# Earlier attention loads, sums and low parts on GpSimd, and two gates moved ahead, in a fused attention and two-FFN kernel

## The chip, the cores and the metric

The kernel runs on one core of one Trainium2 chip. The metric is the device time of one execution in microseconds. PE is the TensorE matmul engine, DVE is VectorE, ACT is ScalarE, POOL is GpSimd and SP is the engine that issues every DMA of this kernel.

## What is computed

Queries, keys and values are (8, 8, 576, 64): 8 sequences, 8 heads, 576 tokens, 64 wide; attention is within chunks of 64 tokens. Its output, 4608 rows of 512, goes through two feed-forward layers:

```python
x  = softmax(q @ k.T / 8) @ v                     # per chunk of 64
xn = (x - mean) / sqrt(var + 1e-6) * g_ln
x  = x + relu(xn @ w_ch1) @ w_ch2                 # 512 -> 2048 -> 512
h  = relu(x @ w_in)                               # 512 -> 1024
c  = sum(conv_w[k] * shift(h, k - 1) for k in range(3))  # along the sequence
out = (h * sigmoid(c)) @ w_out                    # 1024 -> 512
```

## The kernel before, in words

**Precision.** Every large product is done with both operands split into a high part in fp32r and a low part, the rest: `mm3` (L112) is three matmuls (L113 to L115). A high part is one copy on ACT, a low part one subtraction on DVE, both 128x512. The weights come as 64-bit floats and are brought to 32 bits by one ACT step (`a`, L133) and three DVE steps (`t` L139, `m` L145, `n` L151).

**First part (0 to about 490 us): attention and the first layer's `w_ch1`.** 36 tiles of 128 tokens; four tiles make a slab of 512 columns. A slab is multiplied by `w_ch1` by Strassen's scheme: seven products per pair of blocks (`product`, L585), each of 24 matmuls of 256 columns, in a fixed sequence of slots; ACT and DVE take the results out of PSUM (`u`, L611, L615 to L630) and SP stores them to DRAM (`hd`). The attention of the next tiles runs between the slots (`session`, L639). The seven weight operands of each of four blocks (numbers 0 to 3; 0 and 1 for the first half of `w_ch1`'s columns, 2 and 3 for the second) need sums of weight tiles: `Block.s` (L312), four per block.

**Start-up.** The order of the first steps is written out by hand in the table `START`: a letter for the step and a number for the tile or weight. W loads a weight tile, L loads queries and keys (and values) of an attention tile, `a t m n` bring a weight to 32 bits, g scales it by `g_ln` (ACT, L310), s is a Strassen sum, h and l the high and low part; S are a tile's scores (PE, L384), M their maximum (DVE, L400), E the eight exponentials (ACT, L410), R P C V X the rest of attention, B and y the normalisation's statistics (its power of -1/2 is the kernel's one arithmetic step on POOL, L451). What stands behind `|` is placed after slot 0, 1, 2 and so on of the first slab's products, a `/` between slots. Weight n belongs to block n // 4, sum n too; h and l n to block n // 7.

**Second layer (`w_ch2`), about 490 to 886 us.** `Down` p = 0 to 8, one per slab, takes 16 steps in `F_ORDER`; each loads `hr` from DRAM, splits it (`hh` on ACT L701, `hl` on DVE L702) and does 12 matmuls of 512 columns, all into four PSUM banks (even p: banks 0 to 3). The 32 pieces of `w_ch2`, `w_in` and `w_out` are loaded and split meanwhile by `Piece` through `cv_step` (L219), a pipeline of four stages: a, m, h, l. After a pass, `finish` (L773) adds the residual (four DVE adds, L159) and transposes four tiles on DVE into one buffer `x2T` (L779), each stored to DRAM before the next may overwrite it; `load_x2` and `split_x2` (ACT L109, DVE L110) bring the result back as the operand of the second pass.

**Second pass, from 886 us.** For each slab i and each f = 0 to 7 a `Gate` (L881): 12 matmuls into bank 4 + f % 4, then relu (ACT, `hb` L902, `cv` L906), the other two taps of the convolution (DVE, L917), tanh (ACT, L927), the product (DVE, `gt` L932) and its high (ACT, L947) and low part (DVE, L951). `step` (L957) writes these for three gates at a time:

```python
if old:  old.gated(); old.high()
if new:  new.relu()
if new2: new2.taps(); new2.tanh()
if old:  old.low()
```

so a new gate's relu stands on ACT behind the high part of the gate two before it. Split kk of the next slab's operand follows the step of gate f = x0 + kk. `outtile` (L871) is the last matmul with `w_out`.

Of the kernel before, what the change touches and what calls it, by code (L numbers as in the profile page):

```python
# [22 lines left out]
R3 g7 y0 l5 C3 z0 y1 h9 V3 X2 W9 W11 L4 W12 e0 l9 g4 z1 X3 W14 W13 W15 L5 h8  # L23
h7 B2 e1 B3 h6 u1 l7 v1 y3 l8 z3 s4 e3 y2 s6 z2 s5 e2 l6 h11 j0 u2 j1 u3
s7 u5 v3 u7 h10 l11 j2 l10 u6 v2 h12 v6 j3 l12 u4 v5 h13 v4 l13 v7
|
S4 S5 M4 M5 E4 L6 L7 a8 t8 a10 t10 m8 n8
/ E5 g8 a9 t9 m10 n10
/ g10 a11 a12 t11 t12 m9
/ a14 n9 t14 g9 m12  # L30
/ R4 P4 C4 h14 n12 m11 g12 n11 a13
# [13 lines left out]
def attn_moe_moe2(  # L45
# [115 lines left out]
    class Piece:  # L161
# [27 lines left out]
        def l(self):  # L189
            sub(self.dst[:, 1], self.src, self.dst[:, 0].bitcast(F32))  # L190
# [79 lines left out]
    class Block:  # L270
# [53 lines left out]

# [197 lines left out]
    with tc.manual_schedule():  # L522
# [20 lines left out]
        def one(step):  # L543
# [19 lines left out]
            elif kind == "L":  # L563
                at.L(i, late=i > 5)
# [149 lines left out]
        EARLY = 5  # L714
        F_ORDER = [f + 8 * i for f in range(8) for i in range(2)]
        dp = None
        for p in range(NS + 1):
            if p + 1 < NS:
                slabs[p + 1] = Slab(p + 1)
            for G in range(4):  # L720
                for s, (n, lag) in enumerate(SLOTS):
# [15 lines left out]
                    if p == NS - 1:  # L737
                        if (G, s) == (0, 5):
# [7 lines left out]
                            cv_load(2)  # L746
                        elif (G, s) == (2, 5):
# [3 lines left out]
                            cv_load(NF1)  # L751
# [55 lines left out]
        todo = [(p, f) for p in range(NS) for f in F_ORDER]  # L807
        downs = {0: down}
        xrs = {}
        ended = None  # L810
        for n, (p, f) in enumerate(todo):
            hh, hl = parts

            if f >= 8:
                ahead = p * 8 + f % 8 + 3
                if ahead < 8 * NS:
                    if ahead % 8 == 0:
                        downs[ahead // 8] = Down(ahead // 8)
                    downs[ahead // 8].load(ahead % 8)
            if n + 1 < len(todo):  # L820
                parts = downs[todo[n + 1][0]].split(todo[n + 1][1])
            if p == 0 and n % 4 < 3 or n % 2:
                cv_step()
            if ended is not None:
                finish(downs[ended], xrs[ended])
                ended = None
            if f == 4:
                xrs[p] = residual(downs[p])
            if late and f >= 8:
                late.pop(0)()  # L830
            downs[p].down(f, hh, hl)
            if f == NF1 - 1:
                ended = p
            if (p, f) == (0, 15):
                cv_rest()
                load_cw()
                wb_tags = [(wb_p, f"w1{kk}{i}") for kk in range(2) for i in range(7)]
                wb_tags += [(pbx, "wx0"), (pbx, "wx1")]
                for i in range(16):
                    pool, tag = wb_tags[i]  # L840
                    if i < 8:
                        add_wi(i // 4, i % 4, lambda pool=pool: pool, tag)
                    else:
                        add_wo(i - 8, lambda pool=pool: pool, tag)
                cv_load(4)
            if (p, f) == (6, 0):
                load_x2(0)
            if p == 6 and f in (8, 9, 10, 11):
                split_x2(0, f - 8)
        cv_rest()  # L850
        finish(downs[NS - 1], xrs[NS - 1])
        for fn in late:
            fn()
        dp.release()
        wa_p.release()


# [8 lines left out]
        for f in (7, 6, 5):  # L866
            ring(f)
# [165 lines left out]
```

## Time and profile before

| what | value |
|---|---|
| median of 3 runs | 1293.47 us (1290.34 to 1294.29) |
| profiled execution, its own time | 1292.32 us |
| its span, first to last instruction | 1290.5 us |
| PE busy | 1239.9 us, 96% |
| DVE busy | 744.1 us, 58% |
| ACT busy | 613.9 us, 48% |
| POOL busy | 78.0 us, 6% |
| mean granted TensorE clock | 0.976 |

Busy times are sums over the whole span; the stages differ much, so they are read by stage.

### The profile page before, as it was taken

What the parts mean: (1) busy time and instruction counts of PE and PEld (TensorE: products, weight loads), DVE (VectorE), ACT (ScalarE), POOL (GpSimd) and SP (SyncE); (2) the same over time, 40 slices, a digit from 0 to 9 for tenths busy, and PEclk for the clock granted to TensorE, in tenths of its full rate; (3) what the DMA queues carried; (4) which work ended last, traced back from release to release, by engine and by line L of the source; (5) the groups of instructions that cost most, each with busy time, mean ns of one, the idle gap of its engine ahead of it and who ended that gap; (6) DMA issues with size and microseconds to landing.
All of it is one profiled execution on the core that took longest, in us unless ns stands there. A gap on an engine that the chain in (4) does not pass through costs nothing.

```text
span 1290.5 us, 23238 instructions
## 1 busy us (share of the span) xinstructions
PE 1239.9 (96%) x9096; PEld 1080.4 (84%) x9096; DVE 744.1 (58%) x1430; ACT 613.9 (48%) x1510; POOL 78.0 (6%) x172
## 2 busy tenths in 40 slices
PE   5569999999999999999999999999999999999998
PEld 4469999999999987788888888888788888888887
DVE  7897557556565568567633443334875645665540
ACT  6776646556455345244322222222765555565541
POOL 0000000000000000000000000000121111121100
PEclk6589999999999999999999999999999999999999
DMA  9724645555454386676344445440121101211001
GB/s 269 209 103 160 209 160 186 188 175 210 158 197 151 120 284 244 189 269 234 117 143 153 163 155 179 155 162 34 33 66 58 57 18 58 66 38 36 25 25 49
DMA packets 127021, 177.70 MB, mean 138 GB/s; under 512 B 12736, under 2 KB 72128, under 8 KB 126912
## 3 DMA queue, kind: packets, MB, share of 16 engines
q1 hardware_dynamic: 126912, 176.22, 40.8%
q8 instruction: 71, 1.16, 0.4%
q14 instruction: 38, 0.31, 0.1%
HBM read 110.13 MB, written 66.06 MB: 137 GB/s over the span
## 4 chain that ended last, share of the span: by engine, by line
PE 84%; DVE 6%; DMA 5%; ACT 3%; SPq 1%; issue 1%; ACTq 0%; DVEq 0%
PE banks L113 27%; PE banks L114 26%; PE banks L115 26%; PE banks L384 3%; DMA rk<-in_k_dram 1%; DMA w<-in_moe_w_ch_dram 1%; PE banks L466 1%; DVE w L156 1%; PE banks L424 1%; DMA wd<-in_moe_w_ch_dram 1%; DVE hl L702 1%; DMA x2d<-x2T 0%; DVE w L151 0%; DVE u L159 0%; DVE w L145 0%
## 5 line engine op out<-in xcount | busy, mean ns | idle before, releaser
L113 PE MATMUL banks<-xc,w 128*128 128x256 f32 x1008 | 286.7, 284 | 11.2 <-DVE u L159 8.1
L114 PE MATMUL banks<-xc,w 128*128 128x256 f32 x1008 | 281.8, 280 | 0.0
L115 PE MATMUL banks<-xc,w 128*128 128x256 f32 x1008 | 281.7, 279 | 0.0
L701 ACT ACTIVATE hh<-hr 128x512 fp32r<-128x512 f32 x144 | 91.1, 632 | 257.0 <-PE banks L115 256.7
L702 DVE SCALAR_TENSOR_TENSOR hl<-hr,hh 128x512 fp32r<-128x512 f32 x144 | 99.3, 689 | 191.6 <-ACT hh L701 191.5
L113 PEld LDWEIGHTS banks<-xc,w 128*128 128x128 f32 x1008 | 192.1, 191 | 14.4 <-DVE u L159 8.7
L115 PEld LDWEIGHTS banks<-xc,w 128*128 128x128 f32 x1008 | 191.9, 190 | 0.0
L114 PEld LDWEIGHTS banks<-xc,w 128*128 128x128 f32 x1008 | 191.8, 190 | 0.0
L113 PE MATMUL banks<-w,hl 128*128 128x512 f32 x396 | 154.9, 391 | 0.0
L114 PE MATMUL banks<-w,hh 128*128 128x512 f32 x396 | 154.3, 390 | 0.0
L115 PE MATMUL banks<-w,hh 128*128 128x512 f32 x396 | 154.2, 389 | 0.0
L159 DVE TENSOR_TENSOR u<-banks,u 128x512 f32<-128x512 f32 x108 | 74.3, 689 | 113.6 <-ACT u L611 84.9
L917 DVE SCALAR_TENSOR_TENSOR cv<-hb,cw_sb,cv 128x510 f32<-128x510 f32 (+31 forms) x256 | 117.2, 513 | 0.6
L113 PE MATMUL banks<-xb,w 128*128 128x512 f32 x288 | 113.6, 395 | 1.8 <-ACT hb L902 1.4
L114 PE MATMUL banks<-xb,w 128*128 128x512 f32 x288 | 113.1, 393 | 0.0
L115 PE MATMUL banks<-xb,w 128*128 128x512 f32 x288 | 113.0, 392 | 0.0
L611 ACT COPY u<-banks 128x512 f32<-128x512 f32 x108 | 64.4, 596 | 99.4 <-PE banks L115 98.6
L410 ACT ACTIVATE pp<-banks,mx 128x64 f32<-128x64 f32 x288 | 86.8, 335 | 26.4 <-DVE x L438 18.7
L113 PEld LDWEIGHTS banks<-w,hl 128*128 128x128 f32 x396 | 74.4, 188 | 17.7 <-DVE hl L702 2.4
L115 PEld LDWEIGHTS banks<-w,hh 128*128 128x128 f32 x396 | 74.3, 188 | 15.5
L114 PEld LDWEIGHTS banks<-w,hh 128*128 128x128 f32 x396 | 74.3, 188 | 15.2
L904 POOL COPY hal<-hb 128x2 f32<-128x2 f32 x64 | 41.7, 652 | 730.0 <-ACT hb L902 730.0
(106 smaller groups left out, 2184.1 us busy)
## 6 DMA issues: line engine op xcount, KB each, us to landing
hd<-u SPq DMA_DIRECT2D x144, 256.0 KB, 3.2
hr<-hd SPq DMA_DIRECT2D x72, 512.0 KB, 3.7
w<-in_moe_w_ch_dram SPq DMA_DIRECT2D x27, 512.0 KB, 7.4
rv<-in_v_dram SPq DMA_DIRECT2D x36, 256.0 KB, 5.3
xd<-x SPq DMA_DIRECT2D x36, 256.0 KB, 2.2
xr<-xd SPq DMA_DIRECT2D x36, 256.0 KB, 4.2
x2d<-x2T SPq DMA_DIRECT2D x36, 256.0 KB, 2.0
x2r<-x2d SPq DMA_DIRECT2D x36, 256.0 KB, 3.7
```

Source lines behind the costliest of these rows:

```text
L113: nc.tensor.matmul(ps, ll, rh, start=first, stop=False, **kw)
L114: nc.tensor.matmul(ps, lh, rl, start=False, stop=False, **kw)
L115: nc.tensor.matmul(ps, lh, rh, start=False, stop=last, **kw)
L156: nc.vector.tensor_tensor(out=out, in0=a, in1=b, op=ALU.subtract)
L159: nc.vector.tensor_tensor(out=out, in0=a, in1=b, op=ALU.add)
L384: nc.tensor.matmul(ps[half(c), e, j, :], lt[half(e), j, c, :], rt[half(e), j, c, :], start=True, stop=True,)
L410: nc.scalar.activation(out=pp[:, j, e, :], in_=self.both[T][:, e, j, :], func=AF.Exp, scale=SCALE, bias=mx[:, e, j:j + 1], accum_out=sm[:, ...
L611: nc.scalar.copy(flat(t), bank[to])
L701: nc.scalar.activation(out=self.hh, in_=t, func=AF.Relu)
L702: nc.vector.scalar_tensor_tensor(out=self.hl, in0=t, scalar=0.0, in1=self.hh.bitcast(F32), op0=ALU.max, op1=ALU.subtract,)
L904: nc.gpsimd.tensor_copy(out=hal[:, f, :], in_=hb[:, 512:514])
L917: nc.vector.scalar_tensor_tensor(out=cv[:, a:e], in0=hb[:, a + tap:e + tap], scalar=cw_sb[:, tap, f:f + 1], in1=cv[:, a:e], op0=ALU.mult, ...
```

## The change

Five edits. In `START`, the queries and keys of tiles 4 and 5 are loaded before weights 9 and 11 (they were loaded behind 11 and behind 15), their values by new steps K behind weight 15; the scores, maximum and exponentials of tile 5 move from slots 0 and 1 to slot 2. The eight sums of blocks 2 and 3 are issued on GpSimd. The 32 low parts of `Piece` are issued on GpSimd. Loading of the pieces starts with five, then one per step, where it was two, then all of the rest at once. And `Gate(0, 0)` and `Gate(0, 1)` stand within the last down pass, behind its steps of f = 6 and f = 7; the splits of slab 1 move from gates 0 to 3 to gates 2 to 5. For that `hb` and `cv` lie in another pool and `hb` has three buffers instead of four.

```diff
-R3 g7 y0 l5 C3 z0 y1 h9 V3 X2 W9 W11 L4 W12 e0 l9 g4 z1 X3 W14 W13 W15 L5 h8
+R3 g7 y0 l5 C3 z0 y1 h9 V3 X2 L4 W9 L5 W11 e0 l9 g4 z1 X3 W12 W14 W13 W15 K4
+K5 h8 ...
 |
-S4 S5 M4 M5 E4 L6 L7 a8 t8 a10 t10 m8 n8
-/ E5 g8 a9 t9 m10 n10
-/ g10 a11 a12 t11 t12 m9
-/ a14 n9 t14 g9 m12
-/ R4 P4 C4 h14 n12 m11 g12 n11 a13
+S4 M4 E4 a8 t8 a10 t10 m8 n8 L6
+/ g8 a9 t9 m10 n10
+/ S5 M5 E5 g10 a11 a12 t11 t12 m9 L7
+/ R4 P4 C4 a14 n9 t14 g9 m12
+/ h14 n12 m11 g12 n11 a13
...
         def l(self):                                  # Piece
-            sub(self.dst[:, 1], self.src, self.dst[:, 0].bitcast(F32))
+            nc.gpsimd.tensor_tensor(
+                out=self.dst[:, 1], in0=self.src, in1=self.dst[:, 0].bitcast(F32), op=ALU.subtract
+            )
...
         def s(self, i):                               # Block
             y = self.y
+            if self.c:
+                self.s_gp(i)
+                return
...
+        def s_gp(self, i):
+            y = self.y
+            if i == 0:
+                self.sa = self.room(0, [128, 2, 512], F32)
+            if i == 3:
+                self.s4 = at.tile([128, 512], "s4", 1)
+            out, a, b, op = (
+                lambda: (self.sa[:, 0], y[2], y[3], ALU.add),
+                lambda: (self.sa[:, 1], self.sa[:, 0], y[0], ALU.subtract),
+                lambda: (y[2], y[0], y[2], ALU.subtract),
+                lambda: (self.s4, y[1], self.sa[:, 1], ALU.subtract),
+            )[i]()
+            nc.gpsimd.tensor_tensor(out=out, in0=a, in1=b, op=op)
...
-                at.L(i, late=i > 5)
+                at.L(i, late=i > 3)
+            elif kind == "K":
+                at.Lv(i)
...
-                            cv_load(2)
+                            cv_load(EARLY)
...
-                            cv_load(NF1)
+                            cv_load(5)
...
+            if p == NS - 1 and f in (6, 7):
+                step(Gate(0, f - 6))
...
-                self.hb = hb = pb.tile([128, 514], F32, tag="hb", bufs=4, name="hb")
-                self.cv = cv = pb.tile([128, 514], F32, tag="cv", bufs=3, name="cv")
+                self.hb = hb = pbx.tile([128, 514], F32, tag="hb", bufs=3, name="hb")
+                self.cv = cv = pbx.tile([128, 514], F32, tag="cv", bufs=3, name="cv")
...
-            x0 = min(2 * i, 2)
+            x0 = 2
...
-            for f in range(NF2):
+            for f in range(0 if i else BEGUN, NF2):
```

The lines of the changed kernel stand about 20 lower in the first part (L410 is L429, L310 is L312); of the gates, taps L917 is L878, `gt` L932 is L893, `x2T` L779 is L801.

The order of instructions on ACT in the start-up, from tile 4's exponentials on (x8 are the eight of one tile; w are weight tiles), before:

```order
L410 ACTIVATE pp,sm<-banks,mx 128x64 x8
L133 ACTIVATE w_774<-w_449 128x512
L133 ACTIVATE w_777<-w_451 128x512
L410 ACTIVATE pp,sm<-banks,mx 128x64 x8
L310 ACTIVATE w_774<-w_774,g_sb 128x512
L133 ACTIVATE w_774<-w_579 128x512
L310 ACTIVATE w_777<-w_777,g_sb 128x512
```

and in the changed kernel:

```order
L429 ACTIVATE pp,sm<-banks,mx 128x64 x8
L133 ACTIVATE w_743<-w_449 128x512
L133 ACTIVATE w_746<-w_451 128x512
L312 ACTIVATE w_743<-w_743,g_sb 128x512
L133 ACTIVATE w_743<-w_585 128x512
L429 ACTIVATE pp,sm<-banks,mx 128x64 x8
L312 ACTIVATE w_746<-w_746,g_sb 128x512
```

Tile 5's exponentials moved behind g8 and a9; tile 4's still stand ahead of a8 and a10.

POOL's queue of the changed kernel in the first part (rs is the normalisation's power, one per tile; L342 are the sums, L190 the first low parts):

```order
L470 TENSOR_TENSOR rs<-rs,mhalf 128x1 x4
L342 TENSOR_TENSOR w_896<-w_746 128x512
L342 TENSOR_TENSOR w_896<-w_896,w_743 128x512
L470 TENSOR_TENSOR rs<-rs,mhalf 128x1
L342 TENSOR_TENSOR w_746<-w_743,w_746 128x512
L342 TENSOR_TENSOR s_1039<-w_743,w_896 128x512
L470 TENSOR_TENSOR rs<-rs,mhalf 128x1
L342 TENSOR_TENSOR w_1105<-w_840 128x512
L342 TENSOR_TENSOR w_1105<-w_1105,w_807 128x512
L342 TENSOR_TENSOR w_840<-w_807,w_840 128x512
L342 TENSOR_TENSOR s_1149<-w_807,w_1105 128x512
L470 TENSOR_TENSOR rs<-rs,mhalf 128x1 x30
```

Before, this queue held the 36 powers one behind the other; now the sums s8 to s15 stand between the powers of tiles 3, 4, 5 and 6.

DVE where the second pass begins, before (xr are the residual adds of the last down pass, the first L917 the taps of gates 0 and 1):

```order
L159 TENSOR_TENSOR xr<-banks,xr 128x512 x4
L779 STREAM_TRANSPOSE x2T<-xr 128x512 x4
L110 TENSOR_TENSOR xb_10029<-x2r,xb_10027 128x512
L917 SCALAR_TENSOR_TENSOR cv<-hb,cw_sb,cv 128x510
L917 SCALAR_TENSOR_TENSOR cv<-hb,cw_sb,cv 128x511
L110 TENSOR_TENSOR xb_10029<-x2r,xb_10027 128x512
L932 SCALAR_TENSOR_TENSOR gt<-cv,hb 128x511
```

and in the changed kernel:

```order
L878 SCALAR_TENSOR_TENSOR cv<-hb,cw_sb,cv 128x510
L878 SCALAR_TENSOR_TENSOR cv<-hb,cw_sb,cv 128x511
L159 TENSOR_TENSOR xr<-banks,xr 128x512 x4
L801 STREAM_TRANSPOSE x2T<-xr 128x512 x4
L893 SCALAR_TENSOR_TENSOR gt<-cv,hb 128x511
L878 SCALAR_TENSOR_TENSOR cv<-hb,cw_sb,cv 128x510
L878 SCALAR_TENSOR_TENSOR cv<-hb,cw_sb,cv 128x511
L912 TENSOR_TENSOR Gl_10055<-gt,Gh_10054 128x511
L110 TENSOR_TENSOR xb_10066<-x2r,xb_10064 128x512
```

Gate 0's taps moved ahead of the last pass's four transposes; gate 0's product now stands right behind them, and the splits (L110) come two gates later.

## Rows read from the trace of the kernel before

**Rows 1.** The profile's page: busy time, and the chain that ended last.

```profile
PE 1239.9 (96%) x9096; PEld 1080.4 (84%) x9096; DVE 744.1 (58%) x1430; ACT 613.9 (48%) x1510; POOL 78.0 (6%) x172
...
PE 84%; DVE 6%; DMA 5%; ACT 3%; SPq 1%; issue 1%; ACTq 0%; DVEq 0%
```

**Rows 2.** Stages: length; PE, PEld, DVE, ACT, POOL busy; granted clock; DMA share, GB/s.

```profile
0.00:47.00 47.00, 26.95 (x320) 20.45 (x321) 37.28 (x79) 31.65 (x103) 3.62 (x12) 0.59 0.86 239
47.00:101.00 54.00, 34.56 (x495) 32.30 (x494) 46.06 (x92) 38.88 (x117) 1.79 (x2) 0.79 0.45 144
...
455.00:490.00 35.00, 30.21 (x261) 29.62 (x260) 22.55 (x38) 15.56 (x27) 0.00 (x0) 1.00 0.88 317
...
886.00:923.00 37.00, 35.21 (x147) 26.98 (x147) 25.69 (x39) 20.53 (x35) 2.65 (x9) 1.00 0.18 57
```

**Rows 3.** PE, 47 to 102 us: waits; in brackets idle time and its releaser.

```profile
58.05 1.64 PE L384 MATMUL banks<-rk,rq 64*64 64x64 f32 x32 [8.75 <-DMA rk<-in_k_dram]
...
84.27 0.58 PE L113 MATMUL banks<-xc,w 128*128 128x256 f32 x1 [5.36 <-DVE u L159]
...
97.59 2.10 PE L384 MATMUL banks<-rv,pt 64*64 64x64 f32 x64 [3.67 <-ACT pt L430]
```

**Rows 4.** DVE, same stretch: maximum of tile 5, sums s11 and s15.

```profile
59.76 0.69 DVE L400 TENSOR_REDUCE mx<-banks 128x8 f32<-128x512 f32 x1 [3.38 <-PE banks L384]
...
82.93 0.68 DVE L156 TENSOR_TENSOR s<-w,w 128x512 f32<-128x512 f32 x1
...
94.16 0.69 DVE L156 TENSOR_TENSOR s<-w,w 128x512 f32<-128x512 f32 x1
```

**Rows 5.** ACT, same stretch: a8 and a10, and two waits for sums.

```profile
58.80 1.25 ACT L133 ACTIVATE w<-w 128x512 f32<-128x512 f32 x2
...
83.70 0.62 ACT L335 CAST w<-w 128x512 fp32r<-128x512 f32 x1 [1.63 <-DVE s L156]
...
94.94 1.14 ACT L335 CAST w<-w 128x512 fp32r<-128x512 f32 x2 [2.71 <-DVE s L156]
```

**Rows 6.** POOL by line: busy time and mean; then one line's minimum, median, maximum.

```profile
L451 POOL TENSOR_TENSOR rs<-rs,mhalf 128x1 f32<-128x1 f32 x36 | 22.4, 623 | 404.7 <-DVE rs L450 397.2 <-DVE sm L417 7.5
masks.py:199 POOL TENSOR_SCALAR_AFFINE_SELECT ident<-ident 128x128 f32<-128x128 f32 x1 | 0.3, 292 | 0.1
...
L904 POOL COPY hal<-hb x64: 184/924/952, 889.9 to 1210.1; 128x2 f32<-128x2 f32 x64
```

**Rows 7.** PE before a product; DVE's L156 and L702 in the first down pass.

```profile
473.61 0.39 PE L113 MATMUL banks<-xc,w 128*128 128x256 f32 x1 [1.13 <-DVE u L159]
...
506.32 0.68 DVE L156 TENSOR_TENSOR w<-cy,w 128x512 fp32r<-128x512 f32 x1
...
509.32 0.69 DVE L156 TENSOR_TENSOR w<-cy,w 128x512 fp32r<-128x512 f32 x1
...
526.13 0.69 DVE L702 SCALAR_TENSOR_TENSOR hl<-hr,hh 128x512 fp32r<-128x512 f32 x1 [2.03 <-ACT hh L701]
528.85 0.69 DVE L702 SCALAR_TENSOR_TENSOR hl<-hr,hh 128x512 fp32r<-128x512 f32 x1 [2.03 <-ACT hh L701]
```

**Rows 8.** DVE where the second pass begins.

```profile
895.56 0.71 DVE L779 STREAM_TRANSPOSE x2T<-xr 128x512 f32<-128x512 f32 x1 [2.11 <-DMA x2d<-x2T]
...
900.11 0.68 DVE L932 SCALAR_TENSOR_TENSOR gt<-cv,hb 128x511 f32<-128x511 f32 x1
...
904.37 0.68 DVE L932 SCALAR_TENSOR_TENSOR gt<-cv,hb 128x511 f32<-128x511 f32 x1
...
911.77 0.69 DVE L932 SCALAR_TENSOR_TENSOR gt<-cv,hb 128x511 f32<-128x511 f32 x1 [0.41 <-ACT cv L927]
...
914.92 0.69 DVE L932 SCALAR_TENSOR_TENSOR gt<-cv,hb 128x511 f32<-128x511 f32 x1 [0.41 <-ACT cv L927]
```

**Rows 9.** ACT's relu of gates 0 and 2 in the same stretch.

```profile
889.28 0.60 ACT L902 ACTIVATE hb<-banks 128x512 f32<-128x512 f32 x1 [7.61 <-PE banks L115]
...
901.35 0.59 ACT L902 ACTIVATE hb<-banks 128x512 f32<-128x512 f32 x1
```

More of the change, by code (lines that the diff above doesn't have):

```diff
@@ L22 @@
 a7 t7 M2 m7 E2 n5 l3 S3 n6 m4 g5 P2 M3 g6 C2 n4 E3 V2 l4 n7 B1 h5 R2 P3
-R3 g7 y0 l5 C3 z0 y1 h9 V3 X2 W9 W11 L4 W12 e0 l9 g4 z1 X3 W14 W13 W15 L5 h8
-h7 B2 e1 B3 h6 u1 l7 v1 y3 l8 z3 s4 e3 y2 s6 z2 s5 e2 l6 h11 j0 u2 j1 u3
-s7 u5 v3 u7 h10 l11 j2 l10 u6 v2 h12 v6 j3 l12 u4 v5 h13 v4 l13 v7
-|
-S4 S5 M4 M5 E4 L6 L7 a8 t8 a10 t10 m8 n8
-/ E5 g8 a9 t9 m10 n10
-/ g10 a11 a12 t11 t12 m9
-/ a14 n9 t14 g9 m12
-/ R4 P4 C4 h14 n12 m11 g12 n11 a13
+R3 g7 y0 l5 C3 z0 y1 h9 V3 X2 L4 W9 L5 W11 e0 l9 g4 z1 X3 W12 W14 W13 W15 K4
+K5 h8 h7 B2 e1 B3 h6 u1 l7 v1 y3 l8 z3 s4 e3 y2 s6 z2 s5 e2 l6 h11 j0 u2
+j1 u3 s7 u5 v3 u7 h10 l11 j2 l10 u6 v2 h12 v6 j3 l12 u4 v5 h13 v4 l13 v7
+|
+S4 M4 E4 a8 t8 a10 t10 m8 n8 L6
[3 more added lines that the diff above has]
+/ h14 n12 m11 g12 n11 a13
 / R5 P5 C5 l14 t13 g11 m14 h15
@@ L714, in attn_moe_moe2 @@
         EARLY = 5
+        BEGUN = 2
         F_ORDER = [f + 8 * i for f in range(8) for i in range(2)]
@@ L806, in attn_moe_moe2 @@
         xb = [x_parts(pbx, "xb0")]
[L807 to L855, printed above, removed]
-        pb = tc.alloc_tile_pool(name="pb", bufs=1, reuse_waits="tile")
         RING = 1152
         Gh, Gl = {}, {}
-        def ring(f):
-            Gh[f] = pb.tile([128, RING], F32R, name=f"Gh{f}")
-            Gl[f] = pb.tile([128, RING], F32R, name=f"Gl{f}")
-        for f in (7, 6, 5):
-            ring(f)
-        for f in range(5):
-            ring(f)
-        xb.append(x_parts(pb, "xb1"))
         def outtile(T, tail=False):
@@ L969, in step @@
             flow[:] = new, new2
+        todo = [(p, f) for p in range(NS) for f in F_ORDER]
+        downs = {0: down}
+        xrs = {}
+        ended = None
+        for n, (p, f) in enumerate(todo):
+            hh, hl = parts
+            if f >= 8:
+                ahead = p * 8 + f % 8 + 3
+                if ahead < 8 * NS:
+                    if ahead % 8 == 0:
+                        downs[ahead // 8] = Down(ahead // 8)
+                    downs[ahead // 8].load(ahead % 8)
+            if n + 1 < len(todo):
+                parts = downs[todo[n + 1][0]].split(todo[n + 1][1])
+            if p == 0 and n % 4 < 3 or n % 2:
+                cv_step()
+            if ended is not None:
+                finish(downs[ended], xrs[ended])
+                ended = None
+            if f == 4:
+                xrs[p] = residual(downs[p])
+            if late and f >= 8:
+                late.pop(0)()
+            downs[p].down(f, hh, hl)
+            if f == NF1 - 1:
+                ended = p
+            if (p, f) == (0, 15):
+                cv_rest()
+                load_cw()
+                wb_tags = [(wb_p, f"w1{kk}{i}") for kk in range(2) for i in range(7)]
+                wb_tags += [(pbx, "wx0"), (pbx, "wx1")]
+                for i in range(16):
+                    pool, tag = wb_tags[i]
+                    if i < 8:
+                        add_wi(i // 4, i % 4, lambda pool=pool: pool, tag)
+                    else:
+                        add_wo(i - 8, lambda pool=pool: pool, tag)
+                cv_load(4)
+            if p == NS - 1 and f in (6, 7):
+                step(Gate(0, f - 6))
+            if (p, f) == (6, 0):
+                load_x2(0)
+            if p == 6 and f in (8, 9, 10, 11):
+                split_x2(0, f - 8)
@@ new lines, in attn_moe_moe2, with ring @@
+        cv_rest()
+        finish(downs[NS - 1], xrs[NS - 1])
+        for fn in late:
+            fn()
+        dp.release()
+        wa_p.release()
+        pb = tc.alloc_tile_pool(name="pb", bufs=1, reuse_waits="tile")
+        def ring(f):
+            Gh[f] = pb.tile([128, RING], F32R, name=f"Gh{f}")
+            Gl[f] = pb.tile([128, RING], F32R, name=f"Gl{f}")
+        for f in (7, 6, 5):
+            ring(f)
+        for f in range(5):
+            ring(f)
+        xb.append(x_parts(pb, "xb1"))
```

## The prediction

> **What bounds the kernel now.** I read the page first: PE is busy 1239.9 us of a span of 1290.5 and the chain that ended last lies on PE for 84% of the span [rows 1]. So only about 50 us can be won, and a queue that has slack costs nothing. The view by stages says where those 50 us lie [rows 2]: PE lacks 20.05 us before 47 us, 19.44 between 47 and 101, 4.79 between 455 and 490, and 1.79 between 886 and 923; elsewhere it is full but for some four at the very end. The change touches three of these four places, so I cost it stage by stage, each from the queue that PE waits for there.
>
> In the start-up I read PE's waits first, then the two engines that they name. PE sat 8.75 us for tile 5's keys, 5.36 for a DVE addition and 3.67 for an ACT copy [rows 3]. The first looks like the prize, but DVE idled only 3.38 us of it [rows 4]: behind that it runs back to back, 46.06 busy of 54 [rows 2]. DVE and ACT together set this stage, each waiting in turn for the other: ACT waited 1.63 and 2.71 us for the sums s11 and s15, which end on DVE at 83.61 and 94.85 [rows 4, 5].
>
> **Start-up, part by part.** *Loads.* SP issues eight small loads of queries and keys ahead of weights 9 and 11 and two loads of values later. The weights that they pass are wanted from about 60 us on, some ten microseconds behind their landing; nothing on PE, DVE or ACT waits for them. Tile 7's keys now start only behind tile 5's scores in slot 2; they keep a few microseconds. I cost the loads at nothing, with that cover named.
>
> *Tile 5 later.* M4 does not come earlier, since DVE is backlogged before it. With tile 5's maximum gone from there, DVE goes on to a8's conversion, and a8 stands on ACT behind tile 4's exponentials, whose end is at 58.80 [rows 5]. It gets a8 at about 59.45, while before it resumed at 59.76 [rows 4]: of the 3.38 us only 0.3 are won. The rest changes hands: tile 5's exponentials, which filled ACT from 60.76, now stand behind g8 and a9, and g8 waits for DVE's three conversion steps of 0.60 each. Walked on with the same durations, ACT idles about 2.85 us and tile 5's exponentials begin at about 63.95, and everything behind them comes some 1.3 us later.
>
> *Eight sums on GpSimd.* No operation of 128x512 on POOL is in the trace. Its nearest rows are one of 128x128 in 0.292 us and the power on one column in 0.62 us [rows 6]. Four times the columns of the first gives 1.17 us; the bounds are 0.62 (fixed cost alone) and 2.34 (if a second operand costs as much again). I take 1.17, by the row nearest in size. DVE loses 8 x 0.60 = 4.8 us of work, a low price; but the sums are on the path through POOL. s8 and s9 give DVE back 1.2 us, which about cancels the 1.3. s10 and s11 stand on POOL behind tile 4's power, which needs statistics that end at about 82.4 as before: 82.4 + 0.6 + 2 x 1.17 = 85.4 against 83.61, 1.8 us later for the copy that already waited for it [rows 5]. s12 to s15 wait for g15, now at about 90, and end at 90 + 4 x 1.17 = 94.7 against 94.85. Before, three of them ran together from 92.36 in 0.60 each behind other DVE work; now they start earlier and take longer. So the path ends where it did, within a few tenths. At 0.62 per sum it would end 2.2 us earlier, at 2.34 4.7 us later. DVE and POOL at work at once may also disturb each other: POOL's copy of two columns takes 0.184 us at best and 0.924 in the median [rows 6], where DVE works beside it, so POOL at least is held up. I take **+1.0** (−3 to +4.7) for the start-up.
>
> **Between the parts (455 to 520 us).** The wait of 2.06 us for the first piece's load stays, since it comes behind the same three `hr` loads. The wait of 1.13 us for a DVE addition [rows 7] had two low parts of 0.60 ahead of it on DVE; both go to POOL, so it goes. The later wait of 1.60 us has conversion steps ahead of it, which stay. In the first down pass DVE needs 3.00 us per step (506.32 to 509.32), PE 2.72 (526.13 to 528.85) [rows 7]; DVE was the slower one for nine steps but finished within PE's lead, so taking 0.60 of each step off DVE wins nothing there. Loading pieces one by one rather than eleven at once spreads DMA and costs nothing that I find. I take **−1.1** (−1.5 to +5, the upper end from the third rival).
>
> **Where the second pass begins (886 us).** Here is the largest term. Call T0 the end of the last down pass: gate 0's relu starts at 889.28, 2.72 behind it, so T0 = 886.56 [rows 7, 9]. DVE then does the residual adds and four transposes, each waiting 2.11 us for the store of the one before, until 896.27 = T0 + 9.71 [rows 8]. Only then come taps and gate products. PE does not mind: gates 0 to 3 have four free banks, and the relus of gates 0 and 1, which free banks 4 and 5, have no product of an older gate ahead of them on ACT. PE so has six gates, 16.3 us, to cover the transposes. The third relu ends at 901.94, which is 1.83 behind gate 0's product at 900.11 [rows 8, 9]. From there a step takes 4.26 us with a split of the next slab in it and 3.15 without [rows 8]. All in all PE loses little: 147 matmuls of 0.227 are 33.4 of 37.0 us [rows 2], some 3.5 lost.
>
> In the changed kernel gates 0 and 1 lie in the down pass, where ACT and DVE have room; PE's work is the same, the last pass ends at T = T0 + 5.44. The transposes start at T and end at T + 9.75, and gate 0's product stands behind them. The relu of gate 2 stands on ACT behind that product's high part, so it ends at T + 9.75 + 1.83 = T + 11.6. PE has four gates, 10.9 us, to cover this, not six: the two gates that needed nothing of DVE have been spent. Then come four steps with a split (gates 2 to 5, no longer 0 to 3): relus end at T + 15.8, 20.1, 24.4 and 28.6, then 31.8. The last split ends some 2.4 behind the relu of gate 5, at T + 26.8, and slab 1's first gate needs it: it ends at T + 27.5. Three more gates (the last two wait for relus at 28.6 and 31.8, hardly at all) end at T + 27.5 + 3 x 2.72 = T + 35.7. Ten gates are 27.2, so PE loses 8.5 against some 3.5: **+5.0**. Bounds: +3 if PE works on the splits as they come and the pace is nearer to 3.15 (two of the four pauses shrink by 1.1), +7 if TensorE's clock falls in the pauses of up to 4 us, as the granted clock of 0.79 shows for the stage with pauses of 5.36 and 3.67 us [rows 2, 3]. From 923 us on PE is full, so nothing gives this back.
>
> **Sum.** +1.0 − 1.1 + 5.0 = +4.9 on the profiled execution's 1292.32 us, which is 1297.2. That execution is 1.15 below the median shown, 1293.47; against it I say **1298.4 us**, 0.4% slower. About 0.3% (3.9 us) is what a measurement can tell from no change, so 1289.6 to 1297.4 counts as the same.
>
> **Rivals.** *DVE alone sets the start-up.* Then the whole 3.38 us and 8 x 0.60 are won, −8.2: 1293.47 − 8.2 − 1.1 + 5.0 = 1289.2, faster. For it: DVE's 46.06 of 54 us and ACT's waits of 1.63 and 2.71 for DVE's sums. Against it: a8 behind tile 4's exponentials, and g15, which POOL cannot pass. It decides where s15 ends on POOL: before about 91 us instead of 94.7. Chance 0.13.
>
> *The boundary is cheaper.* With +3 there, −2 in the start-up (short sums) and −1.1 it comes to −0.1: 1293.4, no change. For it: PE begins a gate on the first split. Against it: the transposes' end and the pace are measured. Chance 0.32, with the weaker mixtures of it.
>
> *DVE is held up by POOL.* If every DVE step with two operands waits for the POOL operation beside it, eight sums cost DVE 8 x (1.17 − 0.60) = 4.6 us and a down step takes 3.00 − 0.60 + 1.17 = 3.57 against PE's 2.72; nine steps lose 7.7, less the lead of some 2.5, so +5: 1293.47 + 4.6 + 5 + 5 = 1308. For it: POOL's copy of 0.184 that takes 0.924. Against it: no DVE row shows a wait for POOL. Chance 0.10. The Trainium skill (SBUF — State Buffer, Who interferes with whom) says that a DVE instruction with two SBUF inputs contends with a GpSimd instruction that reads SBUF, and that the later one is blocked for the whole of the other. By that rule this rival is the case; the trace agrees for POOL's side only. The GPSIMD Engine Reference (section 3.1) of the Trainium skill has 4497 ns for a sum of 2048 columns; a quarter, 1.12 us as an estimate, would give 94.5 for s15, no other sum.
>
> **How the numbers follow.** My forecast, slower by 2 to 9 us, has 0.45; with the contention rival's 0.10, slower by over 0.3% has 0.55. Within 0.3% 0.32, faster 0.13. The range reaches down to 1290.5, below the case of no change and near to that of the DVE-bound start-up, and up to 1305, between +7 at the boundary with +4.7 in the start-up and the contention case; beyond each end I leave about 1 in 10.
>
> **What would show it.** Start-up: PE's wait of 8.75 gone, tile 5's exponentials near 64, a sum of POOL near 1.17, s15's end near 94.7, PE full from about 101 as before. Middle: the wait of 1.13 gone. Boundary: DVE's gate product right behind the last transpose, PE waiting 8 us in all between the last down pass and gate (1,3). I am wrong if that loss is under 5 us, if s15 ends before 91, or if DVE shows waits for POOL of about a microsecond.

## The result, and the profile after

The changed kernel takes 1311.01 us (median of 4, 1310.39 to 1311.02), the kernel before 1293.3 beside it: ratio 1.0142 (95% interval 1.0129 to 1.0154), 17.7 us slower. I forecast 1298.4 in a range up to 1305. The direction was right, the size was not, and one effect of the other sign was not in the forecast at all.

In some executions, of the kernel before too, the 256-column matmuls of the whole first part follow each other every 117.7 ns instead of 113.5, which adds about 8 us; the traces of start_only and gates_only below are such executions, so their medians are compared and not their spans.

The profiled execution has a span of 1309.2 us against 1290.5. Busy time by stage, columns as in [rows 2], first two stages of the kernel before, which are not shown there:

```profile
490.00:540.00 50.00, 49.53 (x213) 38.55 (x212) 34.33 (x61) 22.88 (x38) 0.00 (x0) 1.00 0.54 171
...
900.00:950.00 50.00, 48.21 (x206) 37.94 (x206) 40.76 (x74) 34.86 (x61) 9.49 (x21) 1.00 0.16 48
```

and the changed kernel:

```profile
47.00:101.00 54.00, 32.97 (x369) 29.94 (x368) 43.75 (x76) 35.17 (x111) 12.86 (x10) 0.79 0.45 147
...
490.00:540.00 50.00, 44.52 (x198) 34.79 (x198) 37.55 (x46) 20.59 (x36) 14.38 (x11) 0.97 0.53 180
...
900.00:950.00 50.00, 43.25 (x173) 33.48 (x172) 33.97 (x55) 24.30 (x43) 4.61 (x13) 0.93 0.13 42
```

PE does less in the start-up, loses 5.5 us between 490 and 540 us (the end of the first part and the first down pass), where it lost half of one, and loses 6.75 where the second pass begins (1.8 before), with a granted clock of 0.93 there.

**Start-up.** PE, DVE, POOL and ACT of the changed kernel, where [rows 3 to 5] stand for the kernel before; the first line of DVE is tile 4's maximum, which began at 55.50 before:

```profile
66.97 1.11 PE L443 MATMUL banks<-ident,pp 128*128 128x128 f32 x4 [5.60 <-ACT pp L429]
...
102.48 0.69 PE L403 MATMUL banks<-rv,pt 64*64 64x64 f32 x32 [3.92 <-ACT pt L449]
```

```profile
56.11 0.69 DVE L419 TENSOR_REDUCE mx<-banks 128x8 f32<-128x512 f32 x1
...
60.16 0.69 DVE L145 SCALAR_TENSOR_TENSOR w<-w,w 128x512 int32<-128x512 int32 x1 [2.49 <-ACT w L133]
...
75.52 1.63 DVE L151 SCALAR_TENSOR_TENSOR w<-w,w 128x512 int32<-128x512 int32 x1
...
86.75 1.64 DVE L151 SCALAR_TENSOR_TENSOR w<-w,w 128x512 int32<-128x512 int32 x1
...
95.72 1.76 DVE L156 TENSOR_TENSOR w<-w,w 128x512 fp32r<-128x512 f32 x1
```

```profile
75.32 1.28 POOL L342 TENSOR_TENSOR w<-w,w 128x512 f32<-128x512 f32 x1
...
86.13 1.71 POOL L342 TENSOR_TENSOR s<-w,w 128x512 f32<-128x512 f32 x1
...
98.22 1.58 POOL L342 TENSOR_TENSOR s<-w,w 128x512 f32<-128x512 f32 x1 [1.30 <-DVE w L156]
```

```profile
87.88 0.62 ACT L354 CAST w<-w 128x512 fp32r<-128x512 f32 x1 [3.93 <-POOL s L342]
...
99.83 1.14 ACT L354 CAST w<-w 128x512 fp32r<-128x512 f32 x2 [3.63 <-POOL s L342]
```

The wait for the keys is gone and DVE waits 2.49 us for a8 instead, much as walked. A sum takes POOL 1.28 us, and up to 1.71 beside DVE; a DVE conversion step that overlaps one takes 1.63 instead of 0.69, a low part up to 1.76. s11 ends at 87.84 (83.61 before) and s15 at 99.80 (94.85). PE's product that waits for ACT's copy `pt` begins at 102.48 (97.59): 4.9 us lost. Of these, 0.6 were lost by tile 4's maximum already, ahead of all that the change moves on DVE; in the runs that leave the start-up as it was, it begins anywhere from 54.8 to 56.8.

**Ahead of the first down pass.** PE's last wait for a DVE addition, in the kernel before and in the changed one, and a conversion step of DVE ahead of it in the changed one:

```profile
487.74 0.39 PE L113 MATMUL banks<-xc,w 128*128 128x256 f32 x1 [1.60 <-DVE u L159]
```

```profile
494.78 0.39 PE L113 MATMUL banks<-xc,w 128*128 128x256 f32 x1 [2.66 <-DVE u L159]
```

```profile
491.09 1.51 DVE L139 TENSOR_SCALAR w<-w 128x512 int32<-128x512 uint32 x1
```

That step took 0.42 before; a low part runs on POOL beside it, and the wait is longer by the same 1.1.

**First down pass.** DVE, POOL and PE, against a step of 3.00 us before [rows 7]:

```profile
507.53 0.68 DVE L723 SCALAR_TENSOR_TENSOR hl<-hr,hh 128x512 fp32r<-128x512 f32 x1
508.13 0.42 DVE L139 TENSOR_SCALAR w<-w 128x512 int32<-128x512 uint32 x1
508.65 1.60 DVE L145 SCALAR_TENSOR_TENSOR cy<-cy,w 128x512 int32<-128x512 int32 x1
510.30 0.69 DVE L151 SCALAR_TENSOR_TENSOR cy<-w,cy 128x512 int32<-128x512 int32 x1
510.90 0.69 DVE L723 SCALAR_TENSOR_TENSOR hl<-hr,hh 128x512 fp32r<-128x512 f32 x1
```

```profile
508.39 1.31 POOL L190 TENSOR_TENSOR w<-cy,w 128x512 fp32r<-128x512 f32 x1 [2.06 <-ACT w L187]
```

```profile
511.64 0.50 PE L113 MATMUL banks<-wd,hl 128*128 128x512 f32 x1 [0.35 <-DVE hl L723]
```

DVE has one operation fewer per step and takes longer: 3.37 us from hl to hl, since L145 takes 1.60 until POOL's low part (508.39 to 509.70) has ended. The residual adds behind the pass begin at 552.50 against 539.36: 13.1 us lost by there, 4.1 of them already at the first product behind a piece's load (468.14 against 464.04). Of the other 9.0, about half are lost before the down pass begins and half in it.

**Where the second pass begins.** DVE, ACT and PE, for [rows 8, 9]:

```profile
905.82 2.73 DVE L159 TENSOR_TENSOR xr<-banks,xr 128x512 f32<-128x512 f32 x4 [3.58 <-PE banks L115]
...
917.30 0.71 DVE L801 STREAM_TRANSPOSE x2T<-xr 128x512 f32<-128x512 f32 x1 [2.11 <-DMA x2d<-x2T]
917.93 0.65 DVE L893 SCALAR_TENSOR_TENSOR gt<-cv,hb 128x511 f32<-128x511 f32 x1
...
922.21 0.68 DVE L893 SCALAR_TENSOR_TENSOR gt<-cv,hb 128x511 f32<-128x511 f32 x1
```

```profile
919.20 0.59 ACT L863 ACTIVATE hb<-banks 128x512 f32<-128x512 f32 x1
```

```profile
919.84 0.50 PE L113 MATMUL banks<-xb,w 128*128 128x512 f32 x1 [1.14 <-ACT hb L863]
...
934.40 0.80 PE L113 MATMUL banks<-xb,w 128*128 128x512 f32 x1 [2.80 <-ACT xb L109]
```

Gate 0's product stands right behind the last transpose, the relu of gate 2 ends 1.86 behind its start, the next step comes 4.28 later, and PE waits for relus and at last for a split. During that last wait of 2.80 us and behind it the granted clock is low for a while:

```profile
935.00:940.00 5.00, 5.00 (x13) 3.89 (x13) 4.52 (x8) 3.47 (x6) 0.28 (x1) 0.55 0.69 192
```

A mean of 0.55 is half speed, 1.2 GHz, for most of these 5 us. The 12 matmuls from 934.40 to 939.79 take 5.4 us, where 12 of 0.227 take 2.7. From 940 us on the granted clock is 1.00 again.

### The profile page after: what moved, and what is told of

The parts are those of the page before. It is cut to its first block, busy times and chain, and to the rows that moved or that the text cites. A ratio compares the mean times of both kernels' runs of the same rounds, so it can differ in the third digit from the quotient of the medians.

```text
span 1309.2 us, 23325 instructions
## 1 busy us (share of the span) xinstructions
PE 1243.9 (95%) x9096; PEld 1084.3 (83%) x9096; DVE 753.6 (58%) x1390; ACT 612.0 (47%) x1510; POOL 130.8 (10%) x212
## 4 chain that ended last, share of the span: by engine, by line
PE 82%; DVE 8%; DMA 4%; ACT 3%; issue 1%; SPq 1%; POOL 0%; DVEq 0%; ACTq 0%; POOLq 0%
PE banks L113 26%; PE banks L114 26%; PE banks L115 26%; PE banks L403 2%; DVE cy L145 1%; PE banks L485 1%; DVE hl L723 1%; DMA rk<-in_k_dram 1%; DMA w<-in_moe_w_ch_dram 1%; PE banks L443 1%; DVE w L139 1%; DVE w L156 1%; DMA wd<-in_moe_w_ch_dram 1%; ACT pp L429 1%; DVE cy L151 1%
## 5 line engine op out<-in xcount | busy, mean ns | idle before, releaser
L878 DVE SCALAR_TENSOR_TENSOR cv<-hb,cw_sb,cv 128x510 f32<-128x510 f32 (+31 forms) x256 | 117.2, 513 | 0.6
L429 ACT ACTIVATE pp<-banks,mx 128x64 f32<-128x64 f32 x288 | 86.9, 337 | 27.4 <-DVE x L457 20.0
```

Of the source, the lines that this page charges most:

```text
L429: nc.scalar.activation(out=pp[:, j, e, :], in_=self.both[T][:, e, j, :], func=AF.Exp, scale=SCALE, bias=mx[:, e, j:j + 1], accum_out=sm[:, ...
L878: nc.vector.scalar_tensor_tensor(out=cv[:, a:e], in0=hb[:, a + tap:e + tap], scalar=cw_sb[:, tap, f:f + 1], in1=cv[:, a:e], op0=ALU.mult, ...
```

## The experiments

**One part back at a time.** These four undo one part of the change, or two:

```diff
# sums_back: no s_gp          # low_back: Piece.l as before
-            if self.c:       -            nc.gpsimd.tensor_tensor(...)
-                self.s_gp(i) +            sub(self.dst[:, 1], self.src, self.dst[:, 0].bitcast(F32))
-                return
# both_back: both             # gates_back:
-        BEGUN = 2
+        BEGUN = 0
...
-            if p == NS - 1 and f in (6, 7):
-                step(Gate(0, f - 6))
-            x0 = 2
+            x0 = min(2 * i, 2)
```

> The changed kernel with the eight sums back on DVE; low parts stay on GpSimd. Theory (GpSimd and DVE hold each other up: a GpSimd sum takes 1.28 us and stretches the DVE step beside it by about as much): s11, which ended at 87.8, ends near 85.5, PE's product behind the copy of pt, which began at 102.5, begins near 99 to 100, and the time falls by 2.5 to 4 us from 1311.0 to 1307 to 1308.5. Rival (the moved exponentials of tile 5 are what is late): it falls by less than 1 us. Second rival (sums are only late, behind the powers in GpSimd's queue): falls too, but then no DVE step of the changed kernel's start-up would have been stretched.

> The changed kernel with the 32 low parts back on DVE; sums stay on GpSimd. Theory (GpSimd holds DVE up): the step of the first down pass takes 3.00 us again, not 3.38, no DVE step of it takes 1.6 us, and the 7 to 9 us lost between 455 and 552 and most of the 2.8 lost in the later down passes come back: 1299.5 to 1302. Rival (the loss there comes from loading pieces one by one, late): falls by less than 2 us, 1309 or more.

> The changed kernel with sums and low parts back on DVE: what is left are the order of the start-up, the loading of pieces and the two gates. Theory: the sum of the other two experiments' gains, so 1296 to 1298; the boundary of the second pass keeps its 2 to 5 us. Rival (the order of the start-up is a gain of its own, 3.38 us of DVE's idle time): 1293 or less.

> The changed kernel with gates 0 and 1 of the first slab and the splits where they were; all else as changed. By my prediction's term the two gates cost 5.0 us: 1306. By the difference of the two traces around the last down pass (the loss is 15.9 us where that pass ends and 18.7 behind the first slab's gates) they cost 2.8: 1308. Rival (the gates are free, the loss there belongs to GpSimd too): 1310.5 or more.

Measured, beside a kernel before of 1291.74 (1.6 lower than beside the changed kernel, so each difference to 1311.0 may be too large by that): sums_back 1307.01 (ratio to before 1.0118, 1.0102 to 1.0133), low_back 1302.06 (1.0074, 1.0058 to 1.0091), both_back 1297.95 (1.0045, 1.003 to 1.006), gates_back 1302.9 (1.0099, 1.0068 to 1.013). So by the medians the sums cost 4.0, the low parts 9.0 and both 13.1: the two add up. The theory held in all three; the order of the start-up is no gain of its own. The gates cost 8.1 and not 2.8: my reckoning from the two traces had missed something that gave 4 to 5 us back behind the same point.

For the start-up the traces say more than the medians. From tile 4's maximum on DVE to PE's product behind `pt` it takes 46.4 us in the three kernels with the sums on GpSimd (the changed one, low_back, gates_back), 43.6 in the three that have the new order and the sums on DVE (sums_back, both_back, start_only), 42.1 in the kernel before and 40.8 to 41.9 in the twelve other runs whose start-up is that of the kernel before. By that point the sums cost 2.8 us and the order 1.5 against the kernel before's trace, up to 2.8 against the others. The stage where the second pass begins, in gates_back:

```profile
900.00:950.00 50.00, 47.21 (x204) 37.47 (x203) 36.37 (x60) 29.43 (x51) 6.66 (x17) 1.00 0.13 42
```

The clock stays at 1.00 there and PE is busy 4 us more than with the early gates.

**One part alone, and GpSimd's work without a result.** start_only takes the new table and the steps K into the kernel before; gates_only the two gates with hb and cv in the other pool; pool_reads and pool_writes leave the low parts on DVE and add GpSimd work that nothing waits for (`junk` is one tile of 240 columns, allocated beside the operands of the down passes); loads_only takes the two numbers of `cv_load`:

```diff
# pool_reads, in Piece.l
             sub(self.dst[:, 1], self.src, self.dst[:, 0].bitcast(F32))
+            for o in (0, 240):
+                nc.gpsimd.tensor_tensor(
+                    out=self.junk, in0=self.src[:, o:o + 240], in1=self.junk, op=ALU.subtract
+                )
# pool_writes, in Piece.l
+            nc.gpsimd.tensor_copy(out=self.junk[:, 0:1], in_=self.src[:, 0:1])
+            for _ in range(4):
+                nc.gpsimd.memset(self.junk, 0.0)
```

> The kernel before with the new order of the start-up and the moved loads of tiles 4 and 5 alone; every sum and low part on DVE. My prediction's walk: DVE waits for a8 behind tile 4's exponentials, ACT idles later, everything some 1.3 us later than before and no sum leaves DVE, so 1.3 to 3 us slower, 1293 to 1295 against 1291.7. From the run with both kinds back on DVE, where PE's product behind pt began 2.5 to 3.5 us later than before: 1294.5 to 1295.5. Rival (the early loads win DVE's idle 3.38 us): 1288.5.

1296.05 against 1293.48, 2.6 more (ratio 1.0009, 0.9979 to 1.0038, so not clear by itself). The rival's gain is not there. In its trace PE's product behind `pt` begins at 98.78, 1.2 later than before [rows 3]; tile 4's maximum stands 0.3 earlier, so that the order costs the 1.5 given above:

```profile
66.05 1.12 PE L424 MATMUL banks<-ident,pp 128*128 128x128 f32 x4 [5.60 <-ACT pp L410]
...
98.78 2.10 PE L384 MATMUL banks<-rv,pt 64*64 64x64 f32 x64 [3.71 <-ACT pt L430]
```

> The kernel before with gates 0 and 1 in the last down pass, the splits two gates later, and hb and cv in the other pool, alone. The gates cost 7.1 us by the comparison of the two traces with and without them; but in every run where hb and cv lie in the other pool the matmuls of the second pass follow each other every 226.6 ns, before every 228 to 232, which is worth some 4.3 us over 357. So 1291.7 + 7.1 - 4.3 = 1294.5. Rival (the shorter pitch comes from something else): 1298 or more. My prediction's term alone (5.0, no gain): 1296.7.

1296.1 against 1293.48, 2.6 more (1.0021, 0.9995 to 1.0046). The theory's 2.8 is nearest, but the interval holds the 5.0 of my term too. The trace decides: from the residual adds of the last but one down pass to the end it takes 448.7 us against 446.3, some 2.5 more (the table further down has the times), and the matmuls of the second pass follow each other every 226.6 ns.

> The kernel before, with every low part still on DVE, and beside each of the 32 low parts two GpSimd subtractions of 240 columns that read the same source and write to an unused tile: GpSimd's work without anything that waits for its result. Theory (GpSimd and DVE exclude each other): DVE steps beside them are stretched, the step of the first down pass goes from 3.00 to 3.8 or more, and the time rises by 6 to 13 us. Rival (the low parts are slow only because the work behind them waits for GpSimd's result): no change, 1291.7.

1307.03 against 1293.48, 13.5 more (1.0085, 1.0058 to 1.0113). DVE and POOL of the first down pass:

```profile
508.42 0.68 DVE L156 TENSOR_TENSOR w<-cy,w 128x512 fp32r<-128x512 f32 x1
509.02 1.18 DVE L706 SCALAR_TENSOR_TENSOR hl<-hr,hh 128x512 fp32r<-128x512 f32 x1
510.13 0.92 DVE L139 TENSOR_SCALAR w<-w 128x512 int32<-128x512 uint32 x1
...
512.49 0.68 DVE L156 TENSOR_TENSOR w<-cy,w 128x512 fp32r<-128x512 f32 x1
```

```profile
508.65 2.12 POOL L192 TENSOR_TENSOR junk<-cy,junk 128x240 f32<-128x240 f32 x2 [1.95 <-DVE cy L151]
```

Nothing waits for these results, and the step still takes 4.07 us (508.42 to 512.49) instead of 3.00. That is the hold-up by itself. No row of DVE there, nor of the changed kernel's down pass, shows a wait for POOL: the hold-up stands in the length of the steps.

> The kernel before, low parts on DVE, and beside each of them GpSimd fills an unused tile of 240 columns four times (after one copy of a single column, which waits for the same source). GpSimd is busy about as long as with the two subtractions, but reads nothing in the fills. If what excludes DVE is GpSimd's reading, no DVE step of the first down pass is stretched by more than 0.3 us and the time is 0 to 5 above the kernel before (the unused tile also moves the addresses of the down pass's operands, which may cost some 3 us of matmul pitch, as in the run with the subtractions: 228.9 ns against 226.6). If any GpSimd work excludes DVE: 8 or more above.

1297.99 against 1292.8, 5.2 more (1.0038, 1.0024 to 1.0052). DVE's step takes 3.16 us, and only L139 is a little longer beside the fills:

```profile
506.97 0.69 DVE L705 SCALAR_TENSOR_TENSOR hl<-hr,hh 128x512 fp32r<-128x512 f32 x1
507.57 0.52 DVE L139 TENSOR_SCALAR w<-w 128x512 int32<-128x512 uint32 x1
508.19 0.69 DVE L145 SCALAR_TENSOR_TENSOR cy<-cy,w 128x512 int32<-128x512 int32 x1
```

```profile
507.15 1.53 POOL L193 MEMSET junk<- 128x240 f32 x4
```

POOL is as busy (1.53 and a copy of 0.51) but reads next to nothing: 8.3 us lie between the two runs, and the stretching by half a microsecond and more with them. Of the 5.2 that remain some 3 go with the unused tile: in both runs the 1728 matmuls of the down passes are 228 to 229 ns apart instead of 226.6. That this comes from the shifted addresses was not run by itself.

> The kernel before with the pieces loaded five at once and then one per step instead of two and then eleven. My prediction costs it at nothing: within 1.5 us of the kernel before. Rival (the change's loads are late and cost part of what is lost between 455 and 552 us): 3 or more slower.

1292.57 against 1292.8 (1.0, 0.9991 to 1.0009): nothing, as costed.

**The address.** One unused tile at the end of the pool of the second pass's operands, of 192, 32 or 2016 bytes:

```diff
+        pbx.tile([128, 48], F32, name="pad")
         pb = tc.alloc_tile_pool(name="pb", bufs=1, reuse_waits="tile")
```

> The kernel before with one unused tile of 192 bytes per partition at the end of the pool that holds the second pass's operands, which moves these operands' addresses by 192 bytes to the same remainder modulo 2048 that they have in the changed kernel; nothing else. Theory (where an operand lies in SBUF sets the pitch of the matmuls that read it): pitch 226.6 ns throughout the second pass and 4 us less, 1287.5. Rival (the pitch in the changed kernel comes from the place of hb and cv, or from hb's three buffers): no change, 1291.7, and the pitch stays at 228 to 232.

> As the run with 192 unused bytes, but with 32: the second pass's operands then begin 64 bytes ahead of a multiple of 2048, where they begin 32 bytes ahead in the kernel before and 224 ahead with 192 bytes. If only the place in the kernel before is bad, the pitch of the second pass's matmuls is 226.6 ns and the time near 1288; if a few steps of 32 bytes are not enough, it stays at 228 to 232 and near 1293.

> As the run with 192 unused bytes, but with 2016, so that the operands begin on a multiple of 2048. If rows that start on such a multiple are the good case, the pitch is 226.6 ns or less and the time near 1288 or below; if what matters is only that the place of the kernel before is left, the same as with 192 bytes.

With 192 bytes it takes 1288.45 against 1293.48 (0.9947, 0.9925 to 0.9968). With 32 bytes it takes 1293.99 and with 2016 bytes 1291.83, in one execution each, against 1292.72; from 960 to 1270 us their traces hold 1348 and 1350 matmuls, as few as the kernel before. The stretch from 960 to 1270 us, first of the kernel before, then of a second run with 192 bytes (pad_b):

```profile
960.00:1270.00 310.00, 310.00 (x1351) 253.15 (x1350) 174.69 (x362) 160.47 (x295) 41.67 (x99) 1.00 0.13 42
```

```profile
960.00:1270.00 310.00, 310.00 (x1369) 256.80 (x1368) 173.00 (x358) 159.94 (x294) 40.91 (x99) 1.00 0.13 43
```

PE is busy all the time in both and does 18 matmuls more in the second: 226.4 against 229.5 ns each. No idle time shows the difference. The starts of the matmuls tell which are slow: in the kernel before they are 233 ns apart where the moving operand lies in that pool (`xb0`, the operand of every other slab, and `wx`, two pieces of `w_out`) and 227 to 229 where it does not; with 192 bytes all are about 227 apart. So some 4.4 to 5 us come from the operands' addresses alone; in the changed kernel they moved because hb and cv came into that pool.

**Without the transposes' wait.** Three of the four transposes behind the last pass write into buffers of `hr`, which the pass has done with; free_T and its repetition free_T_b have the 192 bytes as well, gates_free_T has hb and cv in that place instead, and the early gates:

```diff
-                    x2T = dp.tile([128, 512], F32, tag="x2T", bufs=1, name="x2T")
+                    if free:      # i > 0 and the last pass
+                        x2T = dp.tile([128, 4, 256], F32, tag="hr", bufs=3, name="hr")[:, 0:2]...
+                    else:
+                        x2T = dp.tile([128, 512], F32, tag="x2T", bufs=1, name="x2T")
```

> The kernel before with the 192 unused bytes, and three of the four transposes behind the last down pass written into buffers that the down pass has done with, so that they no longer wait 2.11 us each for the store of the one before. My prediction's working of the boundary: gate 0's product then stands some 5 us earlier, the relus keep ahead of PE, and the 3.5 us that PE loses there go: 3 to 3.5 us below the kernel with the unused bytes alone (1288.45, 5 below the kernel before), so 8 to 8.5 below the kernel before. Rival (the pace of the gates' own steps sets the loss, not the transposes): no more than 5 below.

> The kernel before with the two early gates and the splits two gates later, and the same three transposes without their wait. If the transposes ahead of gate 0's product are what the early gates pay for (my prediction), gate 0's product stands 5.5 us earlier and the cost of the early gates falls from 7 to about 3 us, since the splits still come two gates later: 4 below the run with the two gates alone, so 1 to 2 us below the kernel before. Rival (the late splits are the cost): it stays 2 to 3 us above the kernel before.

> The kernel with 192 unused bytes again, to stand beside the one with the free transposes on the same chip: 5 us below the kernel before.

> The kernel with 192 unused bytes and the three transposes without a wait again. PE's waits behind the last down pass are gone in its trace; by them 2.4 to 3.5 us below the kernel with the unused bytes alone. Rival: the first comparison of the two, from different chips, of 1.5.

free_T 1286.29 (0.9945, 0.9931 to 0.9958) and gates_free_T 1286.75 (0.995, 0.9937 to 0.9964) against 1292.8; on another chip free_T_b 1284.02 (0.9933, 0.9918 to 0.9947) and pad_b 1288.34 (0.9965, 0.9953 to 0.9978) against 1292.72. So the wait of the transposes is worth 4.3 us beside pad_b; the first pair, free_T beside pad, had given only 1.5 (6.5 below the kernel before, where I expected 8 to 8.5), from two chips. And with the wait gone the early gates seem to cost 0.5 us by the medians. The traces settle both: the time from the first residual add behind the last but one down pass (p = 7) to the end holds nothing of what happens ahead of it.

| kernel | first add | span | between |
|---|---|---|---|
| before | 844.24 | 1290.5 | 446.3 |
| changed | 859.91 | 1309.2 | 449.3 |
| gates_back | 858.73 | 1300.7 | 442.0 |
| gates_only | 852.37 | 1301.1 | 448.7 |
| pad | 844.94 | 1286.6 | 441.7 |
| pad_b | 842.60 | 1284.2 | 441.6 |
| free_T | 844.94 | 1282.6 | 437.7 |
| free_T_b | 844.13 | 1281.8 | 437.7 |
| gates_free_T | 844.76 | 1284.9 | 440.1 |

The address is worth 4.6 us (before to pad), the transposes' wait 4.0 (pad to free_T), a little above the 3 to 3.5 that I expected. The early gates cost 7.1 to 7.3 with the wait (pad to gates_only, gates_back to changed) and 2.5 without it (free_T_b to gates_free_T). So two thirds of their cost hang on the transposes, as the first theory has it, and 2.5 us stay, near the 3 that it left for the late splits. PE still waits for a split there, first for ACT's part and then 0.23 us for DVE's:

```profile
912.21 0.49 PE L113 MATMUL banks<-xb,w 128*128 128x512 f32 x1 [1.17 <-ACT xb L109]
```

DVE of free_T behind the last pass, and its stage:

```profile
887.80 0.70 DVE L782 STREAM_TRANSPOSE x2T<-xr 128x512 f32<-128x512 f32 x1
888.42 1.85 DVE L782 STREAM_TRANSPOSE hr<-xr 128x512 f32<-128x512 f32 x3
```

```profile
900.00:950.00 50.00, 50.00 (x222) 41.39 (x221) 41.36 (x77) 35.59 (x62) 10.27 (x22) 1.00 0.19 58
```

The transposes follow each other without a wait, and PE is full from 900 to 950 us. free_T_b is the fastest kernel of the study, 8.7 us below the kernel before and 27 below the changed one.

**A guess that fell.** 64 unused bytes in the pool of the first part's moving operands:

```diff
         su_p.release()
+        xc_p.tile([128, 16], F32, name="padx")
         xc_p.release()
```

> The kernel before with the 192 unused bytes, the three transposes without a wait, and 64 unused bytes in the pool of the first part's moving operands, which brings these to the same remainder modulo 128 bytes as the weights that they meet. In all runs so far the operands of the second pass were fast at a remainder of 32 and slow at 0, 64 and 96; the first part's stand at 96. If the same holds there, the matmuls of 256 columns follow each other every 113.5 ns in the whole first part (in the kernel before some stretches show 116), no execution stands out by 8 us, and the time is 1 to 2 below the run without it: about 10 below the kernel before. Rival (the first part's stretches of 116 have another cause): no difference from the run without it, 8.7 below the kernel before.

1293.5 against 1292.39 (1.0012, 1.0003 to 1.0022), so some 9 slower than free_T_b. Here the remainder of 32 is the slow one: 101 to 455 us hold 4490 PE matmuls, before 4568, and the 256-column ones are 118.6 ns apart throughout. The remainder modulo 128 alone is no rule.

## Why the prediction was wrong, step by step

**Eight sums on GpSimd (in the +1.0 of the start-up): wrong.** The price was near, 1.28 us against 1.17. The step that failed is "DVE loses 8 x 0.60 = 4.8 us of work, a low price", and that I let the hold-up of POOL and DVE stand as a mere possibility. DVE's steps beside the sums are stretched from 0.69 to as much as 1.76, the sums beside them to 1.71. The walk of s12 to s15 shows it: I let them start at 90 and end at 94.7; they started at 92.56, waited 1.30 us for DVE in between and ended at 99.80. Of the 4.9 us lost at 102 us, 0.6 were there at tile 4's maximum, 1.5 are the order (I had walked 1.3) and 2.8 the sums, which I had at next to nothing (4.0 by the medians of sums_back). So the order was right and the sums were wrong; the loss as a whole came out at the bound of +4.7.

**Low parts on GpSimd (−1.1): wrong, and the largest miss.** "Taking 0.60 of each step off DVE wins nothing there" counted only what leaves DVE. Each low part holds one DVE step for 0.9 us, so a step costs 3.37 instead of 3.00 and PE, at 2.72, falls behind for the rest of the pass: +9.0 by low_back, with what is lost ahead of the pass. There the wait of 1.13 did not go either; it is 0.95. Two low parts of 0.60 left DVE's queue ahead of it, but conversion steps in that queue are stretched by a microsecond each. The wait of 1.60, which was to stay, is 2.66. My third rival had this mechanism, at 3.57 per step and 1308 in all, with a chance of 0.10. That was far too little for a case with one row for it (POOL's copy of 0.184 that took 0.924) and only the absence of rows against it. No DVE row showed a wait, and none does in the changed kernel's down pass either, where DVE is held up at every step: I took the hold-up for something that shows as a wait, and it shows only as a longer step. Nothing long ran on POOL before, so no step of the kernel before could be long from it. Of the signs of being wrong that I had named, the third came in that form.

The Trainium skill (SBUF — State Buffer, Who interferes with whom), whose rule stood beside that rival, says that a GpSimd instruction that reads SBUF and a DVE instruction with two SBUF inputs contend, and that the later one is blocked for the whole of the other. The runs agree, both for the reading (pool_reads 13.5 us, pool_writes 5.2) and for the length of the block (L145 0.69 to 1.60 beside a POOL step of 1.31). L139, which has one input, is stretched too, from 0.42 to 0.92 in pool_reads and to 1.51 in the changed kernel.

**Early gates (+5.0, bounds +3 to +7): mechanism right, size short.** Product behind the last transpose, relu 1.86 behind it (1.83 forecast), 4.28 per step with a split (4.26): all as walked. It cost 7.3 by the traces (8.1 by the medians of gates_back, which may be 1.6 too large). What I had put at the upper end happened: the granted clock fell to 0.93 in that stage, while it is 1.00 in gates_back. The 12 slow matmuls behind the last wait cost 2.7 us; without them the term would be 4.6. And gates_free_T shows that the transposes were two thirds of the price, as argued; 2.5 us stay without their wait.

**Moving hb and cv: not costed at all.** I named the other pool in no term, and it moved the addresses of the operands that PE reads. It gave 4.4 to 5 us back, which hid that much of the loss; that the total came out no farther off than it did owes something to this.

**Loads: right** for the pieces (loads_only 0.2 us). The loads of tiles 4 and 5 were never moved without the new order; in the changed kernel nothing on PE, DVE or ACT waits for a weight that they pass.

The parts add up to about the whole. By the medians the order is 2.6 (not clear by itself), the sums 4.0 and the low parts 9.0; by the traces the gates are 7.3 and the address −4.6. That is 18.3 against 17.7, as near as medians that are uncertain by one to two microseconds each, from different chips, let one expect.

## What to carry to other kernels

Moving an operation off a busy engine is costed by what the two engines do to each other, not by what leaves: here 0.60 us taken from DVE cost it 0.9, and a run with much the same work and no reader of its result shows that apart from any dependence. Such a hold-up shows in the length of the steps, not in their waits. Work put ahead in time uses up cover: before moving independent work forward, see which wait it was hiding, and try to remove that wait itself: here that won 4 us, where the move lost 7. And compare the matmul count of stretches in which PE is fully busy; a change of lay-out shows there and in no idle time.

## What the runs showed that I had not expected

Matmuls of 512 columns with their moving operand at another place in SBUF are 226.6 or up to 233 ns apart, the whole second pass more than 1% slower, with PE shown as fully busy. Three places of the second pass's operands were slow; the shift by 192 bytes and the place in the changed kernel were fast; in the first part a shift of 64 bytes made 113.5 ns into 118.6. What property of the address decides is open.
